# One score operation over four banks, and one output operation, for each large attention job

## The chip, the cores and the metric

The kernel runs as one launch on one core of a Trainium2 chip. Its time is the device time in microseconds (us); three runs of the kernel before gave 976.92, 977.61 and 980.19 us, median 977.61. Engines are named as in the profile: PE is TensorE's matmul side and PEld its weight loads, DVE is VectorE, ACT is ScalarE, POOL is GpSimd, SP issues the transfers. PE writes into eight accumulator banks (PSUM) of 512 float32 columns by 128 partitions.

## The reference, cut to what matters

Block-causal attention over 4 batches, 8 heads, 576 positions of width 64, in blocks of 64, then two feed-forward (FF) layers over 2304 tokens, the first with x times sigmoid(x), the second with a leaky slope per column.

```
scores = q @ k^T / 8 ; masked where block(query) < block(key)
attn   = softmax(scores) @ v            # (4, 8, 576, 64) -> (2304, 512)
h = attn @ w_in1 ;  x = (h * sigmoid(h)) @ w_out1
h = x @ w_in2    ;  out = (max(h,0) + alpha*min(h,0)) @ w_out2
```

## The kernel before, in words

Most operands are split into a high and a low part, and each product is three matmuls (high by high, high by low, low by high). Attention is cut into 32 jobs, each for a pair of heads of one batch: 16 small jobs (queries 0 to 255; the first eight of them `FirstJob`) and 16 large ones (`Job` with kind 1: queries 256 to 511 as two tiles of 128 queries, i = 2 and 3, with 384 and 512 keys, and the last 64 queries of both heads as one tile with 576 keys). The first FF layer is cut into chunks of 256 tokens, in steps of 12 matmuls of 128x256, written to the banks `h` (up, `up1`) and `acc` (down, `down1`). The FF matmuls of the tokens that are ready stand between the attention operations of later jobs, so that PE has work while the other engines do the softmax.

A large job's PE operations are these. `bound` (L517, two matmuls of 128x128 into bank `o`) spreads the largest value of v over all partitions. `scores(2)` and `scores(3)` (L539, matmul issued in `product`) make the scores of the two query tiles. Each head's q and k fill 64 partitions, so a score matmul uses 64 of the array's 128 rows, and the two heads' matmuls run as a pair, one in the upper, one in the lower rows, each into its own bank; the profile shows them with the tile 64*128. `last_scores` (L539, all 128 rows, since its q is padded with zeros) makes the scores of the last 64 queries. `output` (L660) multiplies 256 queries' weights by v, and `last_output` (L730) those of the last 64; here one head takes 64 columns of the array, and the profile shows 128*64. All FF matmuls, `bound` and `last_scores` use the whole array, 128*128.

Behind a score operation, for each head DVE writes the mask (L596), takes the row maximum (L598), ACT takes the exponential out of the bank (`p<-e,stat`, with a sum that a following ACTIVATION_READ_ACCUMULATOR reads), DVE makes reciprocals (L623, L626), POOL and DVE make 16-bit parts (L637, L639), and SP issues a transposing transfer into `pT`. The same for the last queries is L681 to L714, with `pT4` as the target. `finish` takes the outputs out of bank `o` (ACT, and DVE L753), or for the last 64 queries through `xf` and a store to `x_last`.

Banks are: `acc` 2, `h` 2, `e` 2, `s` 1, `o` 1. Scores take `e`, `e`, `s` in turn (`ps_scores`).

The order of instructions is set before the program is built. Every step of a job has a due time (`steps`), `Plan.order` walks through all operations with a cost for each, lets an engine take the ready operation with the earliest due time, and gives PE's waits for other engines a slack of 0.56 in large jobs' steps. On the chip every engine then runs its list in that order, and waits where an operand or a bank isn't ready. `after=` (`beside`) keeps one operation behind another in that list; it put `last_output` of a job behind the scores(2) of the second next job, and `last_scores` behind the `output` of the job before.

Of the kernel before, what the change touches and what calls it, by code (L numbers as in the profile page):

```python
# [8 lines left out]
F32 = mybir.dt.float32  # L9
# [5 lines left out]
ALU = mybir.AluOpType  # L15
# [41 lines left out]

BOUND, LATE_OUTPUT, LAST_OUTPUT = NEXT - 1.99, LAST + 1.99, SCORES + 4.01  # L60


class Buf:
# [163 lines left out]
def block_causal_attention_silu_prelu(  # L227
# [238 lines left out]
    class Job:  # L466
# [91 lines left out]
        def scores(self, i):  # L558

            n = 128 * (i + 1)  # L560
            i0 = i % 2
            qk = self.qk
            x = sb(att_p, [128, 10], F32, "stat", 4)
            if i < 2:
                s = ps_scores(self.k)
                views = [(s, lambda r=r: s()[:, r * n:(r + 1) * n]) for r in range(2)]
                for r in range(2):
                    def products(r=r, view=views[r][1]):
                        for f in self.product(view(), slice(0, 128), 256 * r + 128 * i0, 128, 0, n):
                            f()  # L570

                    add("PE", pe_cost(n, n, n), products, [qk], [(s, r)])
            else:
                views = []
                for r in range(2):
                    s = ps_scores(self.k)
                    views.append((s, lambda s=s: s()[:, 0:n]))

                def products():

                    for fs in zip(*(self.product(views[r][1](), slice(64 * r, 64 * r + 64), 128 * i0, 128, 0, n)
                                    for r in range(2))):
                        for f in fs:
                            f()

                self.stands[i] = add("PE", 1.2 * pe_cost(n, n, n), products, [qk], [v[0] for v in views])
            if i < 2:
                s = views[0][0]
                both = lambda: s()[:, 0:2 * n].rearrange("p (r n) -> p r n", r=2)
                add("DVE", dve_cost(128), lambda: nc.vector.memset(both()[0:64, :, n - 64:n], MASKED), [], [s])  # L590
                add("DVE", dve_cost(2 * n), lambda: nc.vector.tensor_reduce(
                    x()[:, 0:2], both(), axis=AX.X, op=ALU.max, negate=True), [s], [(x, 0)])
            else:
                for r in range(2):
# [6 lines left out]
            for r in range(2):  # L601
                s, view = views[r]
# [4 lines left out]
            self.xp[i] = x, p  # L607

        def parts16(self, r):

# [36 lines left out]
                )  # L647

        def output(self):
            base = 2 * self.kind  # L650
            last = base + 1
            o = ps("o")


            def products():
                for kt in range(last + 1):
                    q0 = 128 * max(0, kt - base)
                    for n, (cv, cp) in enumerate(((0, 0), (0, 1), (1, 0))):
                        for r in range(2):
                            nc.tensor.matmul(  # L660
                                o()[64 * r:64 * r + 64, q0:T1], self.v(r, kt, cv), self.pT[r][1]()[:, 2 * kt + cp, q0:T1],
                                start=(kt == 0 and n == 0), stop=(kt == last and n == 2),
                            )

            columns = [T1 - 128 * max(0, kt - base) for kt in range(last + 1)]
            self.stands["output"] = add(
                "PE", 1.1 * pe_cost(*columns * 3), products, [self.pT[0][0], self.pT[1][0], self.v16], [o])
            self.finish(o, T1, self.b + B * self.kind, 0)

        def last_scores(self):  # L670

            qk = self.qk
            x = sb(att_p, [128, 10], F32, "stat", 4, name="stat4")
            s, s2 = ps_scores(self.k), ps_scores(self.k)
            def products():
                for dst, a, b in ((s, 0, 512), (s2, 512, 576)):
                    for f in self.product(dst()[:, 0:b - a], slice(0, 128), 256, 128, a, b):
# [39 lines left out]
            pT = self.pT4 = sb(att_p, [128, 9, 128], F16, "pT4")  # L717
            self.transpose(lambda: pT(), lambda: p16().rearrange("p a m -> p (a m)"), 9, [p16], [pT])

        def last_output(self):  # L720
            pT = self.pT4
            o = ps("o")

            def products():

                runs = [(kt, cv, 2 * kt + cp) for kt in range(4) for cv, cp in ((0, 0), (0, 1), (1, 0))]
                runs += [(4, 0, 8), (4, 1, 8)]
                for kt, cv, run in runs:
                    for r in range(2):
                        nc.tensor.matmul(  # L730
                            o()[64 * r:64 * r + 64, 0:64], self.v(r, kt, cv), pT()[:, run, 64 * r:64 * r + 64],
                            start=(run == 0 and cv == 0), stop=(kt == 4 and cv == 1),
                        )
# [6 lines left out]
        def finish(self, o, w, n, t0):  # L740

            sc, pair = self.sc, self.pair
            scale = lambda: sc()[:, 2:3]
            if n == 2 * B:
                f = sb(att_p, [128, 64], F32, "p4b", 2, name="xf")
                act(w, lambda: f(), lambda: o()[:, 0:w], AF.Copy, [o, (sc, 2)], [f], psum=True, scale=scale)
                dma(lambda: x_last()[pair * 128:pair * 128 + 128, t0:t0 + w], lambda: f(), 32,
                    [f], [(x_last, (pair, t0))])
            else:
                x = x_parts(n)  # L750
                act(w, lambda: x()[:, 0, pair], lambda: o()[:, 0:w], AF.Copy, [o, (sc, 2)], [(x, (0, pair))],
                    psum=True, scale=scale)
                add("DVE", dve_cost(w, 1, 1), lambda: nc.vector.scalar_tensor_tensor(  # L753
                    x()[:, 1, pair], o()[:, 0:w], scale(), x()[:, 0, pair].bitcast(F32),
                    op0=ALU.mult, op1=ALU.subtract), [o, (sc, 2), (x, (0, pair))], [(x, (1, pair))])

        def steps(self):
            i = 2 * self.kind
            steps = [
                (LOAD, self.load), (PREPARE, self.prepare), (BOUND if self.kind else PREPARE + 0.01, self.bound),  # L760
                (PREPARE_V, self.prepare_v),
                (SCORES, lambda: self.scores(i)), (WEIGHTS, lambda: self.weights(i)),
                (SCORES + NEXT, lambda: self.scores(i + 1)), (WEIGHTS + NEXT, lambda: self.weights(i + 1)),
                (LATE_OUTPUT if self.kind else OUTPUT, self.output),
            ]
            if self.kind:
                steps += [
                    (SCORES + LAST, self.last_scores), (WEIGHTS + LAST, self.last_weights),
                    (LAST_OUTPUT, self.last_output),
                ]  # L770
            return steps
# [343 lines left out]
```

## Time and profile before

| | us |
|---|---|
| runs | 976.92, 977.61, 980.19 |
| profiled execution | 975.61 |
| its span, first to last instruction | 973.8 |
| PE busy | 956.1 |
| DVE busy | 597.0 |
| ACT busy | 398.5 |
| POOL busy | 213.8 |

The span is shorter than the execution by 1.8 us, which lie before the first and after the last instruction. Matmuls overlap: the next starts while the one before drains, so the useful length of a matmul is the distance to the next one's end, which the chain of waits gives where PE is its only engine. A row of the chain holds the stretch from the end of the piece before to its own end. Between 190 and 465 us the large jobs run, and PE's list repeats every 16.77 us.

### The profile page before, as it was taken

The page shows a single profiled execution, that of the slowest core. Times are in us where ns is not written, and L with a number is a line of the kernel's source. Part 1 is how long each engine was busy: PE and PEld are TensorE (multiplying, and loading weights), DVE is VectorE, ACT ScalarE, POOL GpSimd, SP SyncE. Part 2 cuts the span into 40 slices and gives each one's busy share as a digit, 9 for nine tenths or more (in the row PEclk, how much of TensorE's full clock was granted, in tenths as well). Part 3 has the DMA queues.
Part 4 walks back from the last instruction along what each step waited for, and adds up shares of the span by engine and source line. Part 5 has one row for each costly group of instructions (what it writes and reads, how often), then busy time and mean ns, then how long its engine had stood idle before and what let it go on. Part 6 is the DMA issues. An engine that isn't in the chain of part 4 may idle for free.

```text
span 973.8 us, 17935 instructions
## 1 busy us (share of the span) xinstructions
PE 956.1 (98%) x7008; PEld 882.4 (91%) x7008; DVE 597.0 (61%) x1343; ACT 398.5 (41%) x928; POOL 213.8 (22%) x262
## 2 busy tenths in 40 slices
PE   7799999999999999999999999999999999999998
PEld 4699999999999999999999999999999999999997
DVE  4899966578877778776113899544443444434443
ACT  7997645455555555553234656211211211211111
POOL 0002313344545445453234200100100100100000
PEclk9999999999999999999999999999999999999999
DMA  9941243356565656564116950010100200000100
GB/s 366 346 198 49 59 115 87 101 111 120 136 143 127 125 129 138 109 133 79 33 55 225 368 209 1 1 66 1 33 33 0 65 1 1 33 1 1 33 1 33
DMA packets 124468, 94.04 MB, mean 97 GB/s; under 512 B 98400, under 2 KB 109792, under 8 KB 124384
## 3 DMA queue, kind: packets, MB, share of 16 engines
q1 hardware_dynamic: 124384, 92.90, 34.4%
q8 instruction: 55, 0.90, 0.4%
q14 instruction: 29, 0.24, 0.1%
HBM read 60.37 MB, written 9.96 MB: 72 GB/s over the span
## 4 chain that ended last, share of the span: by engine, by line
PE 89%; DMA 5%; DVE 3%; ACT 1%; issue 1%; POOL 0%; SPq 0%; POOLq 0%; DVEq 0%; ACTq 0%
PE h L786 29%; PE acc L786 27%; PE e L786 16%; PE s L786 7%; DMA raw0i<-w_in 4%; PE e L539 3%; PE o L660 2%; PE s L539 2%; PE o L730 1%; PE o L517 1%; DMA pT<-p 1%; DVE p L639 1%; DMA raw1i<-w_in 0%; ACT p L301 0%; POOL p L637 0%
## 5 line engine op out<-in xcount | busy, mean ns | idle before, releaser
L786 PE MATMUL h<-xh,w0i 128*128 128x256 f32 x1728 | 229.2, 287 | 1.0 <-DVE w0i L344 0.6
L786 PEld LDWEIGHTS h<-xh,w0i 128*128 128x128 f32 x1728 | 215.8, 193 | 3.5 <-DVE w0i L344 1.0
L786 PE MATMUL acc<-g,w0o 128*128 128x256 f32 x1536 | 201.2, 285 | 0.1
L786 PEld LDWEIGHTS acc<-g,w0o 128*128 128x128 f32 x1536 | 189.7, 192 | 1.6 <-issue 0.5
L301 ACT ACTIVATE g<-u 128x384 fp32r<-128x384 f32 x96 | 50.2, 523 | 270.0 <-DVE u L904 270.0
L786 PE MATMUL e<-w1o,g 128*128 128x512 f32 x576 | 148.8, 394 | 0.0
L786 PEld LDWEIGHTS e<-w1o,g 128*128 128x128 f32 x576 | 106.8, 188 | 16.7
L786 PE MATMUL h<-xh,w1i 128*128 128x384 f32 x576 | 109.1, 337 | 0.0
L786 PE MATMUL acc<-xh,w1i 128*128 128x384 f32 x576 | 108.8, 337 | 0.0
L786 PEld LDWEIGHTS h<-xh,w1i 128*128 128x128 f32 x576 | 102.3, 188 | 4.1
L786 PEld LDWEIGHTS acc<-xh,w1i 128*128 128x128 f32 x576 | 102.4, 188 | 4.0
L311 POOL TENSOR_TENSOR g<-t,g 128x512 fp32r<-128x512 f32 x56 | 77.7, 1387 | 86.6 <-ACT g L301 84.4
L819 DVE SCALAR_TENSOR_TENSOR t<-t,h 128x512 f32<-128x512 f32 x72 | 49.1, 682 | 65.0 <-ACT t L301 64.8
L311 DVE TENSOR_TENSOR g<-u,g 128x384 fp32r<-128x384 f32 x96 | 54.5, 567 | 54.7 <-ACT g L301 54.7
L637 POOL TENSOR_SCALAR p<-p,stat 128x384 f16<-128x384 f32 (+3 forms) x96 | 61.9, 651 | 99.4 <-DVE stat L626 36.4
L786 PE MATMUL s<-w1o,g 128*128 128x512 f32 x288 | 82.0, 393 | 0.0
L311 POOL TENSOR_TENSOR xh<-xs,xh 128x384 fp32r<-128x384 f32 x24 | 25.0, 1071 | 255.0 <-ACT xh L301 255.0
L301 ACT ACTIVATE t<-h 128x512 f32<-128x512 f32 x72 | 43.2, 599 | 82.2 <-PE h L786 77.5
L639 DVE SCALAR_TENSOR_TENSOR p<-p,stat,p 128x384 f16<-128x384 f32 (+3 forms) x96 | 68.6, 730 | 10.4 <-POOL p L637 10.1
L902 DVE TENSOR_SCALAR u<-acc,alpha_sb 128x384 f32<-128x384 f32 x48 | 29.6, 618 | 73.4 <-PE acc L786 73.4
L902 DVE TENSOR_SCALAR u<-h,alpha_sb 128x384 f32<-128x384 f32 x48 | 29.7, 618 | 69.7 <-PE h L786 69.5
L786 PEld LDWEIGHTS s<-w1o,g 128*128 128x128 f32 x288 | 54.1, 188 | 12.5
(113 smaller groups left out, 1154.7 us busy)
## 6 DMA issues: line engine op xcount, KB each, us to landing
st<-qkv_b SPq DMA_DIRECT2D x16, 800.0 KB, 4.7
raw0i<-w_in SPq DMA_DIRECT2D x16, 512.0 KB, 10.2
raw0o<-w_out SPq DMA_DIRECT2D x16, 512.0 KB, 10.2
raw1i<-w_in SPq DMA_DIRECT2D x16, 512.0 KB, 5.7
raw1o<-w_out SPq DMA_DIRECT2D x16, 512.0 KB, 5.6
x<-x2e SPq DMA_DIRECT2D x18, 256.0 KB, 3.4
st<-qkv_first SPq DMA_DIRECT2D x8, 512.0 KB, 8.2
st<-qkv_a SPq DMA_DIRECT2D x8, 512.0 KB, 3.9
```

The lines of the kernel that those rows point to most:

```text
L301: nc.scalar.activation(dst(), src(), func, **k)
L311: eng.tensor_tensor(lo(), src(), hi().bitcast(F32), op=ALU.subtract)
L517: add("PE", 0.25, lambda: nc.tensor.matmul(t()[:, 0:128], am()[:, 0:1].to_broadcast([128, 128]), eye_sb(), start=True, stop=True), [am, ey ...
L539: yield lambda n=n, a=a, b=b: nc.tensor.matmul(dst, w[rows, a, q0:q0 + m], w[rows, b, nq + k0:nq + k1], start=(n == 0), stop=(n == 2))
L637: add("POOL", pool_cost(n), lambda hl=hl, rr=rr, pr=pr: nc.gpsimd.tensor_scalar(hl()[:, :, 0], pr(), rr(), 1.0, op0=ALU.mult, op1=ALU.mult ...
L639: add("DVE", dve_cost(n, 1, 1), lambda hl=hl, rr=rr, pr=pr: nc.vector.scalar_tensor_tensor(hl()[:, :, 1], pr(), rr(), hl()[:, :, 0], op0=A ...
L660: nc.tensor.matmul(o()[64 * r:64 * r + 64, q0:T1], self.v(r, kt, cv), self.pT[r][1]()[:, 2 * kt + cp, q0:T1], start=(kt == 0 and n == 0), ...
L730: nc.tensor.matmul(o()[64 * r:64 * r + 64, 0:64], self.v(r, kt, cv), pT()[:, run, 64 * r:64 * r + 64], start=(run == 0 and cv == 0), stop= ...
L786: nc.tensor.matmul(dst, lhs(a), rhs(b), start=(start and n == 0), stop=(stop and n == 2))
L819: add("DVE", dve_cost(2 * T1), lambda: nc.vector.scalar_tensor_tensor(t(), t(), 1.0, h3(), op0=ALU.add, op1=ALU.mult), [t, h], [t])
L902: add("DVE", dve_cost(T2, 1, 1), lambda: nc.vector.tensor_scalar(u(), h()[:, 0:T2], 0.0, alpha_sb()[:, m:m + 1], op0=ALU.min, op1=ALU.mult ...
```

## The change

A large job's `scores(2)` and `scores(3)` become one PE operation, `row_scores`. It takes four banks at once: `s` and `o` for the tile i = 2, and the two `e` for i = 3. The exponentials (`row_exponents`, `exponents`) still come tile by tile. `last_output` goes: its 28 matmuls stand behind those of `output` in the same operation, and write columns 256 to 319 of the same bank `o`; `finish` gets the first column. `last_scores` takes the two banks `e`. So `s` serves i = 2 alone, and `o` serves `bound`, the second head's scores of i = 2 and the outputs. The number and the sizes of the matmuls stay as they were. `bound` of the next job now goes behind `row_scores` (before: behind `scores(3)`).

```diff
-BOUND, LATE_OUTPUT, LAST_OUTPUT = NEXT - 1.99, LAST + 1.99, SCORES + 4.01
+BOUND, LATE_OUTPUT = NEXT - 1.99, LAST + 1.99
...
                 t()[:, 0:128], am()[:, 0:1].to_broadcast([128, 128]), eye_sb(), start=True, stop=True), [am, eye_sb], [t],
-                after=self.beside(-1, 3))
+                after=self.beside(-1, "scores"))
...
-            else:
-                views = []
-                for r in range(2):
-                    s = ps_scores(self.k)
-                    views.append((s, lambda s=s: s()[:, 0:n]))
-                def products():
-                    for fs in zip(*(self.product(views[r][1](), slice(64 * r, 64 * r + 64), 128 * i0, 128, 0, n)
-                                    for r in range(2))):
-                        for f in fs:
-                            f()
-                self.stands[i] = add("PE", 1.2 * pe_cost(n, n, n), products, [qk], [v[0] for v in views])
...
-            else:
-                for r in range(2):
-                    s, view = views[r]
-                    add("DVE", dve_cost(64), lambda view=view: nc.vector.memset(view()[0:64, n - 64:n], MASKED),
-                        [], [s])
-                    add("DVE", dve_cost(n), lambda view=view, r=r: nc.vector.tensor_reduce(
-                        x()[:, r:r + 1], view(), axis=AX.X, op=ALU.max, negate=True), [s], [(x, 0)])
...
+        def row_scores(self):
+            qk = self.qk
+            tiles = {i: [ps(tag) for tag in tags] for i, tags in ((2, "so"), (3, "ee"))}
+            def products():
+                for i, s in tiles.items():
+                    n = 128 * (i + 1)
+                    for fs in zip(*(self.product(s[r]()[:, 0:n], slice(64 * r, 64 * r + 64), 128 * (i % 2), 128, 0, n)
+                                    for r in range(2))):
+                        for f in fs:
+                            f()
+            self.stands["scores"] = add(
+                "PE", 1.2 * pe_cost(*[384] * 3, *[512] * 3), products, [qk], tiles[2] + tiles[3])
+            self.tiles = tiles
+        def row_exponents(self, i):
+            n = 128 * (i + 1)
+            x = sb(att_p, [128, 10], F32, "stat", 4)
+            views = []
+            for r, s in enumerate(self.tiles[i]):
+                view = lambda s=s: s()[:, 0:n]
+                views.append((s, view))
+                add("DVE", dve_cost(64), lambda view=view: nc.vector.memset(view()[0:64, n - 64:n], MASKED), [], [s])
+                add("DVE", dve_cost(n), lambda view=view, r=r: nc.vector.tensor_reduce(
+                    x()[:, r:r + 1], view(), axis=AX.X, op=ALU.max, negate=True), [s], [(x, 0)])
+            self.exponents(i, n, x, views)
...
-            columns = [T1 - 128 * max(0, kt - base) for kt in range(last + 1)]
+                if not self.kind:
+                    return
+                runs = [(kt, cv, 2 * kt + cp) for kt in range(4) for cv, cp in ((0, 0), (0, 1), (1, 0))]
+                runs += [(4, 0, 8), (4, 1, 8)]
+                for kt, cv, run in runs:
+                    for r in range(2):
+                        nc.tensor.matmul(
+                            o()[64 * r:64 * r + 64, T1:T1 + 64], self.v(r, kt, cv),
+                            self.pT4()[:, run, 64 * r:64 * r + 64],
+                            start=(run == 0 and cv == 0), stop=(kt == 4 and cv == 1),
+                        )
+            columns = [T1 - 128 * max(0, kt - 2 * self.kind) for kt in range(2 * self.kind + 2)] * 3
             self.stands["output"] = add(
-                "PE", 1.1 * pe_cost(*columns * 3), products, [self.pT[0][0], self.pT[1][0], self.v16], [o])
-            self.finish(o, T1, self.b + B * self.kind, 0)
+                "PE", 1.1 * pe_cost(*columns, *[64] * (14 * self.kind)), products, [t for t, _ in pT] + [self.v16], [o])
+            self.finish(o, 0, T1, self.b + B * self.kind, 0)
+            if self.kind:
+                self.finish(o, T1, 64, 2 * B, 64 * self.b)
...
-            s, s2 = ps_scores(self.k), ps_scores(self.k)
+            s, s2 = ps("e"), ps("e")
...
-        def last_output(self):
-            pT = self.pT4
-            o = ps("o")
...
-            plan.at -= 1.0
-            add("PE", pe_cost(*[64] * 14), products, [pT, self.v16], [o], after=self.beside(2, 2))
-            plan.at += 1.0
-            self.finish(o, 64, 2 * B, 64 * self.b)
...
-            i = 2 * self.kind
-            steps = [
-                (LOAD, self.load), (PREPARE, self.prepare), (BOUND if self.kind else PREPARE + 0.01, self.bound),
-                (PREPARE_V, self.prepare_v),
-                (SCORES, lambda: self.scores(i)), (WEIGHTS, lambda: self.weights(i)),
-                (SCORES + NEXT, lambda: self.scores(i + 1)), (WEIGHTS + NEXT, lambda: self.weights(i + 1)),
-                (LATE_OUTPUT if self.kind else OUTPUT, self.output),
+            steps = [(LOAD, self.load), (PREPARE, self.prepare), (PREPARE_V, self.prepare_v)]
+            if self.kind:
+                return steps + [
+                    (BOUND, self.bound), (SCORES, self.row_scores),
+                    (SCORES + 0.01, lambda: self.row_exponents(2)), (WEIGHTS, lambda: self.weights(2)),
+                    (SCORES + NEXT, lambda: self.row_exponents(3)), (WEIGHTS + NEXT, lambda: self.weights(3)),
+                    (SCORES + LAST, self.last_scores), (WEIGHTS + LAST, self.last_weights),
+                    (LATE_OUTPUT, self.output),
+                ]
+            return steps + [
+                (PREPARE + 0.01, self.bound),
+                (SCORES, lambda: self.scores(0)), (WEIGHTS, lambda: self.weights(0)),
+                (SCORES + NEXT, lambda: self.scores(1)), (WEIGHTS + NEXT, lambda: self.weights(1)),
+                (OUTPUT, self.output),
```

On PE, around one large job's scores in the steady part, the list before reads as follows (`h` and `acc` are FF steps, `e` and `s` banks of scores, `pT_5683` the last queries' weights; six score matmuls and 28 of L730 stand there in all, of which the repeats are left out):

```order
L786 MATMUL h<-xh_4180,w0i_1154 128x256 x12
L539 MATMUL e<-qk 128x384
L539 MATMUL s<-qk 128x384
...
L730 LDWEIGHTS v_5396
L730 MATMUL o<-pT_5683,v_5396 64x64
...
L786 MATMUL h<-xh_4180,w0i_1201 128x256 x12
L786 MATMUL acc<-g,w0o_1071 128x256 x12
L786 MATMUL acc<-g,w0o_1108 128x256 x6
L539 MATMUL e<-qk 128x512 x6
L517 MATMUL o<-eye_sb,am 128x128
```

and with the change (line numbers of FF matmuls are two higher there):

```order
L788 MATMUL h<-xh_4209,w0i_1201 128x256 x3
L539 MATMUL s<-qk 128x384
L539 MATMUL o<-qk 128x384
...
L539 MATMUL e<-qk 128x512 x6
L788 MATMUL h<-xh_4209,w0i_1201 128x256 x9
L788 MATMUL acc<-g,w0o_1071 128x256 x12
L788 MATMUL acc<-g,w0o_1108 128x256 x9
L517 MATMUL o<-eye_sb,am 128x128
```

The 384-wide and the 512-wide scores are neighbours now, 15 FF matmuls of `h` stand ahead of them where 12 stood, and `bound` follows 30 FF matmuls later instead of at once. At the outputs the list with the change reads (the first row is the last matmul of the 256 queries, the next two begin those of the last 64, and behind these come the last scores):

```order
L668 MATMUL o<-pT,v_5576 64x128
L678 LDWEIGHTS v_5576
L678 MATMUL o<-pT_5949,v_5576 64x64
...
L539 MATMUL e<-qk 128x512 x3
L539 MATMUL e<-qk 128x64 x3
```

The last queries' outputs have left their place behind the scores, and stand one job earlier, between `output` and `last_scores`. DVE's list behind the scores of i = 2, before (L714 belongs to the last queries, L551 prepares v, `t` is an FF step):

```order
L596 MEMSET e 64x64
L596 MEMSET s 64x64
L598 TENSOR_REDUCE stat<-e 128x1
L714 SCALAR_TENSOR_TENSOR p_5352<-p,stat_5300,p_5352 128x4x128
L714 SCALAR_TENSOR_TENSOR p_5352<-p4b,stat_5300,p_5352 128x64
L551 SCALAR_TENSOR_TENSOR v_5396<-st,sc,v_5396 128x10x64
L598 TENSOR_REDUCE stat<-s 128x1
L819 SCALAR_TENSOR_TENSOR t<-t,h 128x512
```

and with the change (L735 is the former L714, L610 and L611 the mask and the maximum, L821 the former L819):

```order
L735 SCALAR_TENSOR_TENSOR p_5388<-p,stat_5320,p_5388 128x4x128
L735 SCALAR_TENSOR_TENSOR p_5388<-p4b,stat_5320,p_5388 128x64
L610 MEMSET s 64x64
L610 MEMSET o 64x64
L611 TENSOR_REDUCE stat<-s 128x1
L610 MEMSET e 64x64
L611 TENSOR_REDUCE stat<-o 128x1
L611 TENSOR_REDUCE stat<-e 128x1
L821 SCALAR_TENSOR_TENSOR t<-t,h 128x512
```

The two maxima of i = 2 stand side by side now, behind both L735, and L551 has moved away from between them, to the output's place.

## Rows read from the trace of the kernel before

**Rows 1.** The page's part 1: busy us, share of the span, instructions.

```profile
PE 956.1 (98%) x7008; PEld 882.4 (91%) x7008; DVE 597.0 (61%) x1343; ACT 398.5 (41%) x928; POOL 213.8 (22%) x262
```

**Rows 2.** Windows: length, then busy us and instructions of each engine, PEclk.

```profile
299.07:315.84 16.77, 16.77 (x170) 15.45 (x170) 12.92 (x35) 8.81 (x23) 8.09 (x11) 1.00 0.58 133
```

**Rows 3.** Chain of waits, 298.5 to 316 us: start, length, what, matmuls.

```profile
299.07 2.88 PE h L786 x24
...
304.36 2.95 PE acc L786 x24
307.31 1.44 PE h L786 x12
308.74 0.37 PE e L539
...
309.12 0.17 PE e L539
...
309.46 0.56 PE o L730 x28
310.02 1.63 PE h L786 x12
...
313.81 0.90 PE e L539 x6
```

**Rows 4.** Chain of waits, second FF layer, 600 to 612 us.

```profile
603.85 1.39 PE e L786 x6
605.24 0.69 PE s L786 x3
```

**Rows 5.** Chain of waits, 140 to 147.5 us: a small job's scores.

```profile
144.44 0.72 PE s L539 x6
```

**Rows 6.** Timeline of PE: what runs at 309.65 us; start, length, matmuls.

```profile
309.48 0.36 PE L730 MATMUL o<-pT,v 128*64 128x64 f16 x12
```

**Rows 7.** Tile o, 299.07 to 315.84 us: length in ns, minimum, median, maximum.

```profile
L730 PE MATMUL o<-pT,v x28: 195/196/217, 309.4 to 309.8; 128*64 128x64 f16 x28
```

**Rows 8.** Groups by line and form, whole run; the count stands behind x.

```profile
L539 PE MATMUL e<-qk 64*128 64x512 f32 x96 | 15.5, 426 | 0.0
...
L730 PE MATMUL o<-pT,v 128*64 128x64 f16 x448 | 10.1, 198 | 0.0
```

**Rows 9.** Chain of waits, the first large job, 187.5 to 199.5 us.

```profile
192.16 3.06 PE h L786 x24
```

**Rows 10.** Chain of waits, 223 to 228 us, the third large job's scores.

```profile
224.99 0.39 PE s L539
```

**Rows 11.** Timeline of PE, 241.2 to 242.6 us, the fourth large job's scores.

```profile
241.36 0.44 PE L539 MATMUL e<-qk 64*128 64x384 f32 x1
241.94 0.44 PE L539 MATMUL s<-qk 64*128 64x384 f32 x1
```

**Rows 12.** Timeline of ACT, 306 to 324 us: exponentials, last queries, then i = 2.

```profile
308.22 0.20 ACT L301 ACTIVATION_READ_ACCUMULATOR p4b<-e,stat 128x1 f32 x1
...
312.97 0.58 ACT L301 ACTIVATE p<-s,stat 128x384 f32<-128x384 f32 x1
313.45 0.19 ACT L301 ACTIVATION_READ_ACCUMULATOR p<-s,stat 128x1 f32 x1
```

**Rows 13.** Timeline of SP, 306 to 324 us.

```profile
311.63 1.29 SPq L532 DMA_TRANSPOSE pT<-p  x1
```

**Rows 14.** Transfers' issues by line, whole run: count, median us to landing.

```profile
pT<-p SPq DMA_TRANSPOSE x112, 3.1
```

**Rows 15.** Timeline of DVE, 306 to 324 us: two row maxima.

```profile
312.32 0.55 DVE L598 TENSOR_REDUCE stat<-s 128x1 f32<-128x384 f32 x1
...
314.93 0.69 DVE L598 TENSOR_REDUCE stat<-e 128x1 f32<-128x512 f32 x1
```

**Rows 16.** Chain of waits behind the attention, 515 to 570 us.

```profile
521.60 4.78 DMA raw1i<-w_in
```

More of the change, by code (lines that the diff above doesn't have):

```diff
@@ L587, in scores @@
[L587 to L592, printed above, removed]
-            else:
-                for r in range(2):
-                    s, view = views[r]
-                    add("DVE", dve_cost(64), lambda view=view: nc.vector.memset(view()[0:64, n - 64:n], MASKED),
-                        [], [s])
-                    add("DVE", dve_cost(n), lambda view=view, r=r: nc.vector.tensor_reduce(
-                        x()[:, r:r + 1], view(), axis=AX.X, op=ALU.max, negate=True), [s], [(x, 0)])
+            s = ps_scores(self.k)
@@ new lines, in scores, with products @@
+            both = lambda: s()[:, 0:2 * n].rearrange("p (r n) -> p r n", r=2)
+            for r in range(2):
+                def products(r=r):
+                    for f in self.product(both()[:, r], slice(0, 128), 256 * r + 128 * i, 128, 0, n):
+                        f()
+                add("PE", pe_cost(n, n, n), products, [qk], [(s, r)])
+            x = sb(att_p, [128, 10], F32, "stat", 4)
+            add("DVE", dve_cost(128), lambda: nc.vector.memset(both()[0:64, :, n - 64:n], MASKED), [], [s])
@@ L600, in scores, with exponents @@
+            add("DVE", dve_cost(2 * n), lambda: nc.vector.tensor_reduce(
+                x()[:, 0:2], both(), axis=AX.X, op=ALU.max, negate=True), [s], [(x, 0)])
+            self.exponents(i, n, x, [(s, lambda r=r: both()[:, r]) for r in range(2)])
+        def exponents(self, i, n, x, views):
             p = []
-            for r in range(2):
-                s, view = views[r]
+            for r, (s, view) in enumerate(views):
                 pr = sb(att_p, [128, 512], F32, "p", 3)
@@ L649, in output @@
         def output(self):
-            base = 2 * self.kind
-            last = base + 1
             o = ps("o")
+            pT = self.pT
+            if self.kind:
+                pT = pT + [(self.pT4, None)]
             def products():
+                base = 2 * self.kind
+                last = base + 1
                 for kt in range(last + 1):
@@ L660, in products @@
                             nc.tensor.matmul(
[L661 removed]
+                                o()[64 * r:64 * r + 64, q0:T1], self.v(r, kt, cv), pT[r][1]()[:, 2 * kt + cp, q0:T1],
                                 start=(kt == 0 and n == 0), stop=(kt == last and n == 2),
                             )
[L665 removed]
+                if not self.kind:
[3 more added lines that the diff above has]
+                for kt, cv, run in runs:
+                    for r in range(2):
+                        nc.tensor.matmul(
[4 more added lines that the diff above has]
+            columns = [T1 - 128 * max(0, kt - 2 * self.kind) for kt in range(2 * self.kind + 2)] * 3
             self.stands["output"] = add(
[L667 to L668 removed]
+                "PE", 1.1 * pe_cost(*columns, *[64] * (14 * self.kind)), products, [t for t, _ in pT] + [self.v16], [o])
+            self.finish(o, 0, T1, self.b + B * self.kind, 0)
+            if self.kind:
+                self.finish(o, T1, 64, 2 * B, 64 * self.b)
         def last_scores(self):
@@ L718, in last_weights, with finish @@
             self.transpose(lambda: pT(), lambda: p16().rearrange("p a m -> p (a m)"), 9, [p16], [pT])
-        def last_output(self):
-            pT = self.pT4
-            o = ps("o")
[L724 to L733, printed above, removed]
-            plan.at -= 1.0
-            add("PE", pe_cost(*[64] * 14), products, [pT, self.v16], [o], after=self.beside(2, 2))
-            plan.at += 1.0
-            self.finish(o, 64, 2 * B, 64 * self.b)
-        def finish(self, o, w, n, t0):
+        def finish(self, o, at, w, n, t0):
             sc, pair = self.sc, self.pair
@@ L750, in finish @@
                 x = x_parts(n)
-                act(w, lambda: x()[:, 0, pair], lambda: o()[:, 0:w], AF.Copy, [o, (sc, 2)], [(x, (0, pair))],
+                act(w, lambda: x()[:, 0, pair], lambda: o()[:, at:at + w], AF.Copy, [o, (sc, 2)], [(x, (0, pair))],
                     psum=True, scale=scale)
                 add("DVE", dve_cost(w, 1, 1), lambda: nc.vector.scalar_tensor_tensor(
-                    x()[:, 1, pair], o()[:, 0:w], scale(), x()[:, 0, pair].bitcast(F32),
+                    x()[:, 1, pair], o()[:, at:at + w], scale(), x()[:, 0, pair].bitcast(F32),
@@ L766, in steps @@
[L766 to L771, printed above, removed]
+            steps = [(LOAD, self.load), (PREPARE, self.prepare), (PREPARE_V, self.prepare_v)]
+            if self.kind:
+                return steps + [
[5 more added lines that the diff above has]
+                ]
```

11 lines of the change are left out of this document (2 added, 9 removed).

## The prediction, made before the change was run

> **What bounds the kernel now.** I read the page's busy shares first: PE is busy 956.1 of 973.8 us, DVE 597.0, ACT 398.5 [rows 1]. Then the stretch of the large jobs: in one turn of PE's list, 16.77 us, PE has no idle time, while DVE is busy 12.92 us and ACT 8.81 [rows 2]. So the chain of waits there runs along PE alone, and each of its rows is the time PE needs for that piece. In it 24 FF matmuls take 2.88 us, 0.12 each [rows 3]. The pieces that use half the array stand out, and so do the pieces behind them: 12 FF matmuls behind L730 take 1.63 us, where 12 others take 1.44 [rows 3]. Something is paid where PE goes from one cut of the array to another, and the change takes such places away. The clock is at its higher level throughout (PEclk 1.00 in [rows 2]), so it is no term.
>
> **The change part by part.** The matmuls stay; what goes is three seams in each steady job.
>
> (a) The second entry into the 64-row cut. The three pairs of 512 columns took 0.90 us [rows 3]. Three whole-array matmuls of 512 columns take 0.69, 0.23 each [rows 4], and the two halves of a pair run together. So 0.90 - 0.69 = 0.21 is the entry. The same from the other operation: its first pair took 0.37, the next 0.17 [rows 3], so 0.20. I take 0.20. There are 96 such matmuls, 6 for each of 16 jobs [rows 8]: 16 x 0.20 = 3.2 us. In the joined operation the 512-wide pairs follow the 384-wide ones in the same cut.
>
> (b) The way back from L730 to the whole array: 1.63 - 1.44 = 0.19 [rows 3], for 16 jobs (448 matmuls, 28 each [rows 8]): 3.0 us. The way back from `output` stays, now behind the last queries' part.
>
> (c) The entry into L730. Its 28 matmuls took 0.56 us [rows 3]. At one moment 12 of them run [rows 6], each for 0.196 us [rows 7], so one comes every 0.0163 us, and 28 need 0.46; the entry is 0.10. 16 jobs: 1.6 us. Behind `output` they stand in the same cut.
>
> (d) In the first two large jobs there is no L730 yet behind scores(2), which therefore pays its own way back: 24 FF matmuls behind it take 3.06 instead of 2.88 [rows 9], 0.18 each, 0.36 us. That goes too.
>
> Sum of a to d: 8.2 us. Per steady job it is 0.49, so a turn should take 16.28 instead of 16.77.
>
> The seams inside the joined operations aren't in this trace. Bounds: nothing, as where whole-array matmuls go from bank to bank (6 and 3 matmuls of 512 columns take 1.39 and 0.69, the same each [rows 4]), and 0.20 from (a). I take nothing, the row in which bank and operands change and the cut doesn't. The Trainium skill (TensorEngine Tiling (Array Packing), Tiling Modes, Key Properties) says that changing the mode, not just the tile, drains TensorE; by that too the new seams are free. The 0.20 and 0.10 above are this kernel's measures of such drains.
>
> (e) Waits that are there now. Row scores of the third job waited 0.39 - 0.01, about 0.38 us, for the exponential of the last queries, which held bank `s` [rows 10]; in the fourth it was 241.94 - 241.36 = 0.58 [rows 11]. With the change the banks of the last queries are the two `e`, which the scores reach with their fourth pair only, 0.7 us later, and 15 FF matmuls stand ahead where 15 or 18 stood. That should take away 0 to 0.96 us. On the other side, the order puts only 24 + 6 FF matmuls between last scores and new scores in the second job, where 24 + 18 stood: it arrives 12 x 0.12 = 1.4 us sooner, less the 0.7 that the `e` are reached later, so 0 to 0.7 us is lost there, once. Together between 0.96 gained and 0.7 lost; I take 0.5 gained, nearer to the two rows than to the unshown loss.
>
> New waits in the steady part, each against the time at which PE arrives:
> Bank `o` for `bound`. Now `bound` takes `o` while nothing of the scores is in it; with the change it must wait until the second head's exponential has left `o`. Today that exponential's last piece ends at 313.45 + 0.19 = 313.64 [rows 12], 4.90 us behind the FF matmul ahead of the scores, which ended at 308.74 [rows 3]. With the change PE comes to `bound` after 0.71 (384-wide), 0.69 (512-wide), 0.18 (way back as in d) and 30 FF matmuls, 3.60: 5.18 us. It is in time by 0.28. Moreover the second maximum now stands beside the first, with L551 no longer between. I take a wait of zero; bounds 0 and 0.55 + 0.69 = 1.24 us minus 0.28, 0.96, a job, if two maxima more had to be done first [rows 15]. Behind `bound` in PE's list is everything, so that such a wait is paid in full.
> Banks `e` for the 512-wide scores: last exponentials end at 308.22 + 0.20, that is 4.06 us behind the last scores' end at 304.36 [rows 3, 12]. PE comes there after 2.95 + 15 x 0.12 + 0.71 = 5.46. In time by 1.4.
> The last queries' weights for the joined output: the transfer is issued at 311.63 [rows 13], and at a median of 3.1 us [rows 14] lands at 314.73, 10.4 us behind the last scores' end. The joined output stands a further 57 FF matmuls behind the scores, so PE comes there after 2.95 + 1.80 + 1.58 + 6.84 = 13.2 us, plus 1.27 for `output` itself. In time by 3 us or more. A transposing transfer that has to queue behind another costs one issue more, 1.29 us, and is hidden by that.
> `v` for a later job is prepared when the joined output is done, about a job earlier than now; this gives time and takes none on PE.
> DVE, ACT, POOL and SP do the same work as before; a turn shorter by 0.49 leaves DVE at 12.92 of 16.28, so it bounds nothing as a sum.
>
> Behind the attention the first FF layer's rest and the second layer follow. The chain has one stretch off PE there, a weight transfer of 4.78 us [rows 16], into a place that PE's own last reading of older weights sets free; it moves along with PE. So what is won before 470 us arrives at the end.
>
> Sum: 8.2 + 0.5 = 8.7. The profiled execution took 975.6 us, its span 973.8; that makes 966.9 for such an execution. The median of the runs is 977.6, 2.0 above it; I take the difference against the median: 968.9 us.
>
> **The rivals.**
> Emptying the banks takes over (slower). Four banks are now filled within 1.4 us, and `bound` stands 30 FF matmuls behind. If the exponential out of `o` comes behind three maxima, and the FF tanh that ACT has ahead of it in its list comes late as well, it ends 1.24 us later than today, and PE waits 0.96 us in each of 15 jobs: 14.4 us lost against 8.2 won, 983.8 us. It decides from 8.2/15 = 0.55 us of wait a job. For it: the margin is only 0.28 us, and the order sets both L735 ahead of both maxima. Against it: DVE has 3.9 us free in a turn, ACT 8.0 [rows 2], and the second exponential's start today comes behind L551, which leaves. The Trainium skill speaks for it (the same page, Performance Considerations, PSUM Bottleneck: tiling speeds up TensorE but not the emptying, which may become the bound); by the busy times of this trace it does not.
> A part is eaten by waits. The margin at `bound` fails by a quarter of a microsecond: 15 x 0.25 = 3.8 us, so 8.2 - 3.8 = 4.4 gained, 973.2 us. For it: the same margin of 0.28; the shares of DVE and POOL are uneven from job to job, and the waits of [rows 10, 11] show that the slack in the plan was overrun twice.
> The change doesn't do what it says: the price is one of starting a 64-row or 64-column piece on new banks or operands, not of changing the cut. Then a and c stay and only b and d go: 3.4 us, 974.2 us. Against it: six whole-array score matmuls in their own bank between FF steps take 0.72, 0.12 each, with no start price [rows 5].
>
> **How the numbers follow.** My forecast, a to d with e between its bounds: 0.80; its own range is 8.2 + 1.0 to 8.2 - 0.7 gained, 968.4 to 970.1, and with the runs' scatter (0.7 below and 2.6 above the median) 967.5 to 971.5. Part eaten 0.10; doesn't do what it says 0.05; emptying takes over 0.03; a wait that eats all and leaves it equal 0.02. For 8 in 10 the range has to hold the forecast and most of the next case: 966.5 to 973.0. A measurement of this kernel tells 0.3% (2.9 us) from no change. Faster: 0.80 + 0.10 + most of the third, 0.93; within: 0.04; slower: 0.03.
>
> **What would show it.** A turn of PE's list of 16.3 us; in the chain the six 512-wide matmuls in about 0.69 us without an entry, the last queries' 28 in about 0.46, one long way back of 0.19 behind each joined operation, and no L-line of another engine between. Wrong it would be if the page's waits name ACT or DVE ahead of L517 or L539 with more than some tenths of a microsecond a job, or if the 512-wide pairs still take 0.90.

## The result and the profile after

The changed kernel took 984.53 us (median of 6 runs, 983.28 to 985.51), the one before 977.3 in the same comparison: a ratio of 1.0073, 95% interval 1.0055 to 1.0091. Slower by 0.7%, where the prediction had 968.9 us and faster. The number is close to the first rival's 983.8, but its place is another one.

The busy shares of the changed kernel (us, share, instructions), beside [rows 1]:

```profile
PE 955.8 (97%) x7008; PEld 884.9 (90%) x7008; DVE 612.2 (62%) x1343; ACT 393.5 (40%) x928; POOL 214.1 (22%) x262
```

PE is busy as long as before in a span that is 7.7 us longer. Its window over four turns, where [rows 2] had 16.77 for one (length, then busy us and instructions of PE, PEld, DVE, ACT, POOL; clock, DMA share, GB/s):

```profile
303.40:373.25 69.85, 67.32 (x675) 62.42 (x674) 57.64 (x138) 34.36 (x89) 32.14 (x41) 1.00 0.64 127
```

A turn is 69.85/4 = 17.46 us. PE stands idle 0.63 us in it and is busy 16.83, no less than the 16.77 of before; the clock is unchanged (1.00). Who is waited for, PE's rows of the waits between 200 and 470 us (us in total, times, longest):

```profile
PE e L539 <- ACT p L301: 8.6, 10, 1.2
```

That is the first 512-wide matmul of the joined scores, held by the exponentials of the last queries, which have to leave the banks `e`. It comes in 10 of the last 13 large jobs. The chain of waits over one such place, beside [rows 3] (start, length, what, matmuls):

```profile
323.29 0.90 PE e L539 x3
324.19 0.39 issue
324.59 0.84 DVE p L645
325.43 0.37 issue
325.79 0.47 DVE xh L754
326.27 1.45 DVE v L551
327.71 0.60 DVE stat L702
328.31 0.47 DVE qk L504
328.78 0.13 DVE stat L704
328.92 0.67 DVE qk L507
329.58 0.08 DVE stat L706
...
329.75 0.79 ACT p L301 x2
...
330.58 1.03 PE e L539 x3
```

At 324.19 the first, 512-wide three of the last queries' six score matmuls end, and the chain leaves PE: it runs through DVE to the maximum of those scores (L702 to L706) and through ACT, and comes back to PE at 330.58. The 64-wide three end a little later, as PE's timeline shows:

```profile
323.22 1.22 PE L539 MATMUL e<-qk 128*128 128x512 f32 x6
```

So the last scores end at 324.44; in [rows 3] their end, with the 64-wide ones, is 304.36. ACT behind them, beside [rows 12]:

```profile
329.75 0.69 ACT L301 ACTIVATE p<-e,stat 128x512 f32<-128x512 f32 x1 [3.30 <-DVE stat L706]
...
330.62 0.20 ACT L301 ACTIVATION_READ_ACCUMULATOR p4b<-e,stat 128x1 f32 x1
```

The banks are empty at 330.82, 6.38 us behind the last scores; before it was 4.06. Why shows in DVE's timeline of the kernel before, around its last scores' end at 304.36:

```profile
303.21 1.41 DVE L639 SCALAR_TENSOR_TENSOR p<-p,stat,p 128x512 f16<-128x512 f32 x2
304.54 0.48 DVE L753 SCALAR_TENSOR_TENSOR xh<-o,sc,xh 128x256 fp32r<-128x256 f32 x1
304.94 0.68 DVE L681 TENSOR_REDUCE stat<-s 128x1 f32<-128x512 f32 x1
```

and of the changed one, around 324.44 (L645 is the former L639, L754 the former L753, L702 the former L681):

```profile
323.49 2.38 DVE L645 SCALAR_TENSOR_TENSOR p<-p,stat,p 128x512 f16<-128x512 f32 x2 [0.18 <-POOL p L643]
325.79 0.47 DVE L754 SCALAR_TENSOR_TENSOR xh<-o,sc,xh 128x256 fp32r<-128x256 f32 x1
326.19 1.53 DVE L551 SCALAR_TENSOR_TENSOR v<-st,sc,v 128x640 f16<-128x640 f32 x1
327.64 0.68 DVE L702 TENSOR_REDUCE stat<-e 128x1 f32<-128x512 f32 x1
```

The maximum starts 3.20 us behind the scores instead of 0.58. Of these 2.62 us 1.45 are L551 (its row in the chain), which now stands ahead of it: its buffer of `v` comes free with the joined output, a job earlier, so the planner takes it sooner. The rest is L645 and L754, which end later against the scores; the two L645 alone take 2.38 us where the two L639 took 1.41. The matmuls pay a second time: the second bank comes free later than the first, and the three pairs, which run side by side when both banks are free, get out of step. From the first's start to the last's end they take 1.25 us, where they take 0.86 in an order without this wait (shown below):

```profile
330.58 1.25 PE L539 MATMUL e<-qk 64*128 64x512 f32 x6 [0.67 <-ACT p L301]
```

### The profile page after: what moved, and what is told of

Read it like the earlier page. It is cut to its first block, busy times and chain, and to the rows that moved or that the text cites. A ratio compares the mean times of both kernels' runs of the same rounds, so it can differ in the third digit from the quotient of the medians.

```text
span 981.5 us, 17936 instructions
## 1 busy us (share of the span) xinstructions
PE 955.8 (97%) x7008; PEld 884.9 (90%) x7008; DVE 612.2 (62%) x1343; ACT 393.5 (40%) x928; POOL 214.1 (22%) x262
## 4 chain that ended last, share of the span: by engine, by line
PE 78%; DVE 10%; ACT 5%; issue 3%; DMA 2%; POOL 1%; SPq 0%; POOLq 0%; ACTq 0%; DVEq 0%
PE h L788 26%; PE acc L788 22%; PE e L788 16%; PE s L788 7%; ACT p L301 3%; PE e L539 3%; PE o L668 2%; DVE v L551 2%; DVE p L645 2%; DMA raw0o<-w_out 1%; PE s L539 1%; DVE stat L611 1%; DVE stat L702 1%; POOL p L643 1%; DMA pT<-p 1%
## 5 line engine op out<-in xcount | busy, mean ns | idle before, releaser
L311 POOL TENSOR_TENSOR g<-t,g 128x512 fp32r<-128x512 f32 x56 | 79.8, 1424 | 125.9 <-ACT g L301 89.0
L311 DVE TENSOR_TENSOR g<-u,g 128x384 fp32r<-128x384 f32 x96 | 54.5, 567 | 54.4 <-ACT g L301 54.4
L645 DVE SCALAR_TENSOR_TENSOR p<-p,stat,p 128x384 f16<-128x384 f32 (+3 forms) x96 | 77.1, 831 | 17.5 <-POOL p L643 17.2
L821 DVE SCALAR_TENSOR_TENSOR t<-t,h 128x512 f32<-128x512 f32 x72 | 48.9, 679 | 53.3 <-ACT t L301 51.8
L311 POOL TENSOR_TENSOR xh<-xs,xh 128x384 fp32r<-128x384 f32 x24 | 25.0, 1070 | 255.0 <-ACT xh L301 255.0
L301 ACT ACTIVATE p<-e,stat 128x512 f32<-128x512 f32 (+2 forms) x78 | 46.8, 605 | 75.7 <-DVE stat L706 41.5
L643 POOL TENSOR_SCALAR p<-p,stat 128x384 f16<-128x384 f32 (+3 forms) x96 | 57.6, 610 | 79.1 <-DVE stat L632 28.8
```

The costliest lines, as they stand in the source:

```text
L301: nc.scalar.activation(dst(), src(), func, **k)
L311: eng.tensor_tensor(lo(), src(), hi().bitcast(F32), op=ALU.subtract)
L643: add("POOL", pool_cost(n), lambda hl=hl, rr=rr, pr=pr: nc.gpsimd.tensor_scalar(hl()[:, :, 0], pr(), rr(), 1.0, op0=ALU.mult, op1=ALU.mult ...
L645: add("DVE", dve_cost(n, 1, 1), lambda hl=hl, rr=rr, pr=pr: nc.vector.scalar_tensor_tensor(hl()[:, :, 1], pr(), rr(), hl()[:, :, 0], op0=A ...
L821: add("DVE", dve_cost(2 * T1), lambda: nc.vector.scalar_tensor_tensor(t(), t(), 1.0, h3(), op0=ALU.add, op1=ALU.mult), [t, h], [t])
```

## The experiments

Three theories stood against each other. A, waits of place: the seams are worth what was priced, and the waits come from where the planner puts instructions; it reckons with DVE durations that are too short (0.80 us for L551, measured 1.52 in most jobs) and puts the scores to the very moment at which it thinks their banks free. B: the round of the other engines (emptying four banks, `p`'s three buffers) has become the bound, and no order helps. C: the joined output itself costs the time. The kernel before ran again beside each group of experiments, with medians from 976.1 to 976.9 us; the ratios are to those.

**One instruction moved back.** L551 behind the last maxima:

```diff
-                [st, (sc, 0), (v16, 0)], [(v16, 1)])
+                [st, (sc, 0), (v16, 0)], [(v16, 1)], after=self.beside(-1, "last"))
...
-            add("DVE", dve_cost(80), lambda: nc.vector.tensor_tensor(
+            self.stands["last"] = add("DVE", dve_cost(80), lambda: nc.vector.tensor_tensor(
```

> The changed kernel, and in its order the preparation of v (L551, DVE) is kept behind the maxima of the last queries (L702 to L706). Theory A (the four-bank scores wait for the last queries' exponentials because L551, 1.45 to 1.53 us there, stands ahead of those maxima in DVE's list): the exponentials end about 1.5 us sooner behind the last scores, but the order also moves the scores 6 to 12 FF matmuls (0.7 to 1.4 us) forward, so a part of the wait stays; 972 to 980 us. Theory B (emptying four banks at once and the three exponential tiles p are the bound, whatever the order): 982 to 986 us, the wait per job as large as now. Theory C (the joined output is the cause): 983 to 986 us.

979.78 us, ratio 1.0038 [1.0024, 1.0051], at the upper end of A. PE's waits between 200 and 470 us:

```profile
PE o L517 <- ACT p L301: 1.4, 4, 0.5
PE e L539 <- ACT p L301: 0.4, 1, 0.4
```

Against the kernel before, 3.6 us are lost (979.78 - 976.2) instead of 7.2; the turn is 17.1 us. The banks are empty 4.35 us behind the last scores (326.81 and 322.46 in the job at 326 us), near the 4.06 of before. But with L551 the planner also moved the scores, in most jobs to 27 FF matmuls behind the last scores instead of 39. PE comes to them after 4.10 us, with little idle time, and still ahead of the second bank:

```profile
326.56 1.26 PE L539 MATMUL e<-qk 64*128 64x512 f32 x6
```

So L551's place is a cause; what it costs besides is hidden from the list of waits, which shows idle time alone.

**Only the price corrected.** Nothing but the planner's number for L551:

```diff
-            add("DVE", dve_cost(64 * nv, 1, 1), lambda: ...
+            add("DVE", 1.5 if self.kind else dve_cost(64 * nv, 1, 1), lambda: ...
```

> The changed kernel with one number altered: the planner reckons a large job's v low parts (L551) at 1.5 us, what the changed kernel's trace has for it (1.45 to 1.53), in place of 0.80; nothing else, and no margin on banks. L551 stays where the planner wants it. By theory A (waits of place: the scores are placed to the moment at which the planner thinks their banks free, and it thinks too early) the 512-wide scores now stand 45 feed-forward matmuls behind the last scores in place of 36 to 42, so 0.36 to 1.1 us later; of the 1.0 to 1.57 us waits some 0.3 to 0.6 stay: 973 to 979 us. By theory B (the other engines' round is the bound) the time stays at 981 to 986. By theory C (the joined output itself costs it) 981 to 986.

977.98 us, ratio 1.0009 [0.9998, 1.0021]; within A, and not told apart from the kernel before. L551 still takes 1.52 us in most jobs of this trace, but the planner, knowing it, puts the scores 6 to 9 FF matmuls later, and no idle time is left there. Waits have opened at the next bank:

```profile
PE o L517 <- ACT p L301: 5.0, 10, 0.5
```

**Margins instead.** Places later than the planner thinks the bank free. For the scores:

```diff
-                        o.ready = max(o.ready, old.free_at + 0.2)
+                        o.ready = max(o.ready, old.free_at + 0.2 + (o.extra if o.engine == "PE" else 0.0))
...
-                "PE", 1.2 * pe_cost(*[384] * 3, *[512] * 3), products, [qk], tiles[2] + tiles[3])
+                "PE", 1.2 * pe_cost(*[384] * 3, *[512] * 3), products, [qk], tiles[2] + tiles[3], extra=1.5)
```

and in a second kernel for the bound's maximum too:

```diff
-                after=self.beside(-1, "scores"))
+                after=self.beside(-1, "scores"), extra=1.2 * self.kind)
```

> The changed kernel, with 1.5 us added in the order's reckoning to the moment at which the banks are free for the joined scores; nothing else. In the steady part 24 + 27 FF matmuls instead of 24 + 15 stand between last scores and joined scores, 1.4 us more. Theory A (a wait of place: the order has no slack on banks): most of the wait of 1.0 to 1.5 us goes, and the seams' 8.2 us come through: 968 to 973 us. Theory B (a bound by the other engines' round): the wait moves along with the scores, or comes up at bound; 981 to 986 us.

> As e4 (joined scores 1.5 us later in the order's reckoning), and bound of the large jobs reckoned 1.2 us later as well. In e4 the wait at the 512-wide scores was gone and eight waits of 0.9 us had come up at bound, for bank o's exponential. Theory A (waits of place at two banks; seams as priced): both go, 968 to 971 us. Theory B (the other engines' round per job is the bound): the wait comes up at a third place, at the outputs or at FF matmuls, and the time stays at 974 to 977 us.

Scores alone: 975.29 us, ratio 0.9992 [0.9982, 1.0001], a miss for A and for B, between their ranges. The wait at the scores is gone, one at the bound has taken its place, as B had said:

```profile
PE o L517 <- ACT p L301: 6.0, 8, 0.8
```

Both: 968.11 us, ratio 0.9911 [0.9894, 0.9928], within A and faster than both kernels. Of PE's waits between 200 and 470 us one row is left:

```profile
PE o L668 <- DVE largest L520: 1.5, 3, 0.5
```

B is refuted by this: the same work on every engine, four banks filled at once, and PE waits 1.5 us in all.

**Both cures.** L551 behind as above, with the bound 1.2 us later and the scores 1.0 or 1.5 us later.

> As e1 (L551 behind the maxima of the last queries), with the joined scores reckoned 1.0 us later and bound 1.2 us later. 24 + 12 to 24 + 15 FF matmuls stand between last scores and joined scores, as in the changed kernel itself, so that against it mainly L551's place differs. Theory A: the exponentials are there in time, 967 to 971 us. Theory B: 974 us and more.

> As e6 with 1.5 us in place of 1.0 us at the joined scores. Theory A: no wait is left to take away, so the same as e6 within 1 us. Theory B: as e6.

969.68 us (0.9931 [0.9914, 0.9948]) and 969.13 (0.9919 [0.99, 0.9939]), both within A. Once the banks are hardly waited for, neither L551's place nor half a microsecond of margin makes a difference that these runs can tell.

**The price and the bound's margin.** L551 priced at 1.5, the bound 1.2 us later, no margin at the scores.

> The changed kernel with L551 priced at 1.5 us as in the run with that one number altered (977.98 us; in its trace 10 waits of the bound's maximum for bank o, 5.0 us in sum on the engine, the turn 17.3 us at each), and besides the bound's maximum placed 1.2 us later for a large job; no margin at the scores. By theory A those ten waits are what is left: starts of bound come about 0.78 us after the matmul before them instead of 0.12, so some 6.6 us go, and the time is 970 to 974 us, near the 968 to 970 of the orders that placed scores and bound by margins. By theory B (the other engines' round is the bound, 17.3 us a turn) it stays at 976 to 980.

968.83 us, ratio 0.9913 [0.9892, 0.9933]. Better than A's range. The planner moved L551 too: in the job below it stands behind the first of the last queries' maxima and takes 0.93 us. The window over four turns:

```profile
318.91:383.97 65.06, 65.06 (x673) 61.66 (x672) 54.45 (x138) 34.53 (x90) 31.51 (x40) 1.00 0.67 137
```

65.06/4 = 16.27 us a turn without idle time of PE, where the prediction had 16.28. The chain of waits through one turn names PE alone:

```profile
351.51 1.27 PE o L668 x24
352.78 0.44 PE o L678 x28
353.22 1.15 PE e L539 x6
354.37 2.96 PE acc L788 x24
357.33 2.52 PE h L788 x21
359.84 0.37 PE s L539
...
360.56 0.70 PE e L539 x4
361.26 0.55 PE h L788 x3
```

and in PE's timeline the 512-wide pairs, in step:

```profile
360.40 0.86 PE L539 MATMUL e<-qk 64*128 64x512 f32 x6
```

**Each half by itself.** First the joined scores with the last queries' output kept as an operation of its own, then the joined output with the scores of before (of the first edit, the line that puts the operation back into the job's steps):

```diff
...
-                    (LATE_OUTPUT, self.output),
+                    (LATE_OUTPUT, self.output), (SCORES + 4.01, self.last_output),
...
```

> Only the joined scores over four banks; the last queries' output is an operation of its own again, behind the scores of the second next job. It saves one of the 0.2 us entries a job, 3.2 us, and L551 is back behind the scores, as its buffer comes free later; but the scores stand only 24 + 3 to 24 + 6 FF matmuls behind the last scores. Theory A: the wait at the 512-wide scores is 0.3 to 1.0 us a job from the closer place alone; 977 to 986 us. Theory B: 983 to 990 us. Theory C: 973 to 976 us.

> Only the joined output; scores(2) and scores(3) stay two operations with banks e, e, s in turn. By the prices of the seams it saves 0.10 us a job, 1.6 us. L551 moves ahead of the last queries' maxima here too. Theory A: the last exponentials are late here as well, and scores(2) waits for bank s or e, up to 1 us a job; 976 to 986 us. Theory B: no four-bank operation, no wait; 974 to 977 us. Theory C: 982 us and more.

Scores alone: 996.35 us, ratio 1.021 [1.0181, 1.024], above all three ranges, ten above A's. PE waited 9.9 us for the banks `e`, 12 times, up to 2.3 us. At the longest the chain is:

```profile
305.02 1.63 DVE v L551
306.65 0.03 DVE largest L522
306.68 6.38 DMA st<-qkv_b
...
313.14 0.84 ACT qk L301 x2
```

L551 is the last reader of the loaded rows `st`; the load for a later job waits for it, and ACT's copy of that load stands in ACT's list ahead of the exponentials that empty the banks. Output alone: 984.36 us, ratio 1.0088 [1.0066, 1.011], within A's range but within C's as well, with the same kind of wait at bank `s`:

```profile
PE s L539 <- ACT p L301: 5.2, 10, 1.6
```

Then each half with L551 behind and margins: the joined output with both scores 1.0 us later, the same with the joined output itself 1.2 us later as well, and the joined scores 1.5 us later.

> As e3 (only the joined output), with L551 kept behind the maxima of the last queries and the first scores of a large job reckoned 1.0 us later. Theory A: the loss of e3 (8 us) came from L551's new place and the order's missing slack on banks; it goes, and the seam's 0.10 us a job is left: 973 to 976.5 us. Theory C (the joined output itself costs): 980 us and more.

> The joined output alone, with L551 behind the last maxima and the scores 1.0 us later, as in the run before it of this kind, and besides the joined output itself stands 1.2 us later behind the bound's maximum, which uses the same bank o. In that earlier run the trace had 10 waits of 0.7 to 1.2 us, 8.0 us in sum, of the joined output for the bound's maximum (L520), and 983.79 us. By theory A the waits go and the joined output's seams come through (terms b, c and half of d, 4.8 us): 971 to 975 us. By theory C (the joined output itself costs it) it stays at 979 to 985.

> The joined scores alone (the last output stays an operation of its own, with its own turn of bank o), with L551 behind the last maxima and the joined scores 1.5 us later. With the joined scores alone and nothing moved the run had 996.35 us and 12 waits of up to 2.3 us, 9.9 us in sum, for banks e. By theory A these go and the entry of the second scores (term a, 3.2 us) comes through, with up to 1 us of waits at the last output: 972 to 977 us. By theory B (emptying four banks at once is the bound) 983 or more.

All three missed A's ranges: 983.79 us (1.0071 [1.0056, 1.0086]), which lies in C's; 990.38 (1.0125 [1.011, 1.014]), above C's; and 981.84 (1.0039 [1.0025, 1.0053]), between A's and B's. In each, most of the waits that were meant went and others came, the largest for DVE or ACT. PE's largest rows between 60 and 480 us, of the first:

```profile
PE o L663 <- DVE largest L520: 8.0, 12, 1.0
```

of the second:

```profile
PE h L782 <- DVE xh L750: 6.1, 3, 2.5
PE o L663 <- DVE largest L520: 2.1, 2, 1.5
```

and of the third:

```profile
PE o L666 <- DVE largest L520: 4.5, 8, 0.9
PE o L736 <- ACT p L301: 3.0, 5, 0.7
```

In the first, the joined output waits for the reading of the bound's maximum out of the same bank `o`, 15 to 21 FF matmuls earlier in PE's list, which on DVE stands behind a row maximum. In the second this is down to 2 times, but FF input (`xh`) now ends behind two weight parts on DVE, up to 2.5 us late. C isn't shown by them, since the same joined output runs with few waits or none in the four orders of 968 to 970 us above; but that either half alone wins its share isn't shown either, and stays open.

## Why the prediction was wrong

**The step that failed** is "Banks `e` for the 512-wide scores ... In time by 1.4." It took the 4.06 us from the scores to empty banks from the trace of before, for an order in which that distance isn't the same: it is 6.38. The new order has L551 ahead of the last maxima, and I had read of it only that L551 leaves the place between the first and second maximum, and that its earlier preparation "takes none on PE". PE came to the 512-wide scores 330.58 - 0.67 - 324.44 = 5.47 us behind the last scores, as reckoned (5.46); it was the second bank's emptying that came 0.9 us behind PE instead of 1.4 ahead of it. That L551's place and its price have a part in this is shown: with L551 moved back the distance is 4.35 and the loss against the kernel before 3.6 us instead of 7.2, with its price corrected 1.1. That the two L645 take longer, too, is read from the trace; no run tests it alone.

**Bank `o` for `bound`, "in time by 0.28", wait of zero.** In the changed kernel this holds only because PE is late already. Where the scores no longer wait, the bound does: 8 times with margin at the scores, 10 times with the price corrected, and moving it is worth 975.29 - 968.11 = 7.2 us and 977.98 - 968.83 = 9.2 (medians of different comparisons, good to about 1 us). Of these two waits in a row the first hides the second.

**Seams, a to d, 8.2 us: right.** Without idle time the turn is 16.27 us (forecast 16.28). The pieces agree: the six 384-wide scores take 360.56 - 359.84 = 0.72 and the 512-wide ones behind them 0.70, without the entry that (a) took from 0.90; the last queries' 28 take 0.44, with (c) gone; three FF matmuls behind the joined scores take 0.55, that is 0.19 more than 0.36, the way back. The new seams inside the joined operations cost nothing. The rule of the Trainium skill (TensorEngine Tiling (Array Packing), Tiling Modes, Key Properties), that a drain goes with a change of mode, not of tile, is borne out by these rows. The four orders with 1.5 us of bank waits or less between 200 and 470 us, 968.11 to 969.68 us, stand where the prediction stood (968.9).

**The loss in numbers.** The changed kernel's starts of the joined output between 233.58 and 443.67 us are 12 turns of 17.51, each 1.24 above 16.27. At the place shown, 0.67 us of idle time and 1.25 instead of 0.70 make up 1.22 of it. Added up over the 16 jobs of the trace, the stretch from the end of the 384-wide scores to that of the 512-wide ones is 26.4 us, where 16 x 0.70 are 11.2: 15.2 us lost, of which the list of waits names 8.6. With L551 moved back the same sum is 7.5 us too long, with its price corrected 2.9, with the margin at the scores nothing. So 8.2 us were won and 15.2 given back, 7.0 us slower; measured are 984.53 - 977.3 = 7.2.

**The joined output's weights, "in time by 3 us or more"**, and DVE, ACT and POOL not bound as sums: held. **(e)**, a half microsecond once, can't be told apart from the new waits. The rival "Emptying takes over" had the sign and, by chance, the size; its bank, and its reason (more maxima ahead of the one on `o`), were not those of the trace. A chance of 0.03 for slower was far too small for a sum that stood on margins of 0.28 and 1.4 us. One sum of the forecast is off: 968.4 - 0.7 and 970.1 + 2.6 make 967.7 to 972.7, not 967.5 to 971.5; against 984.53 this changes nothing.

## What to carry to other kernels

Where a change takes time off the engine that bounds, the distances of the old trace (from a bank's filling to its emptying) hold only if the engines that empty it run the same instructions in between: read the new order there on each of them, with measured durations, before a margin is subtracted. A buffer that comes free earlier isn't free of cost: a planner uses it at once, and may put the work that it allows ahead of something urgent. A list of waits shows idle time alone: matmuls that get out of step because one bank comes late count as busy, and what the list left out was nearly half of the loss here. And a wait that is taken away may only uncover the next one, so the cure is to be tried on the pair: here the wait at the scores alone taken away (by a margin or by the right price) brought the kernel back to where it was before, the bound's as well brought 0.9%.

## What the runs showed of the hardware

L551's duration depends on what POOL is doing. The groups by line and form, 200 to 440 us (count, busy us, mean ns; idle before), of the kernel before:

```profile
L551 DVE SCALAR_TENSOR_TENSOR v<-st,sc,v 128x640 f16<-128x640 f32 x14 | 12.4, 884 | 1.0 <-POOL v L548 1.0
```

of the changed kernel:

```profile
L551 DVE SCALAR_TENSOR_TENSOR v<-st,sc,v 128x640 f16<-128x640 f32 x14 | 18.2, 1299 | 0.0
```

and of the one with both margins:

```profile
L551 DVE SCALAR_TENSOR_TENSOR v<-st,sc,v 128x640 f16<-128x640 f32 x15 | 13.1, 870 | 0.0
```

Of the changed kernel's long ones, the one at 326.19 took 1.53 us. POOL's timeline there has an instruction that had begun before it, the second of these:

```profile
324.10 1.23 POOL L548 TENSOR_SCALAR v<-st,sc 128x640 f16<-128x640 f32 x1
325.30 1.73 POOL L311 TENSOR_TENSOR g<-t,g 128x512 fp32r<-128x512 f32 x1
```

The Trainium skill (SBUF — State Buffer, SBUF: two separate sides) says that DVE with two inputs from SBUF and POOL share a port as a lock: whoever starts first has it, the other waits. The rows agree: L551 started 0.89 us into L311 and ended 0.69 us behind its end at 327.03. So do all fourteen traces: of the large jobs' L551, the 127 that start while POOL is idle take 0.87 to 0.89 us, and the 97 that start inside a POOL instruction end 0.67 to 0.69 us behind that one's end, however long that makes them, 0.92 us or 1.95. The two L645 fit as well: the second ended at 325.87, 0.54 us behind the end of L548, which prepares `v` too. No run moves the POOL instruction alone. It means that an instruction's price depends on its place, and moving it changes both.
